# Experts on the tokens that chose them, instead of every expert on every token

## The chip, the cores and the metric

The kernel runs on one core of a Trainium2 chip. The metric is device time in microseconds (us). The kernel before takes 2458.44 us, the median of two timed runs (2458.17 and 2458.72). TensorE is called PE here, VectorE DVE, ScalarE ACT, GpSimd POOL and the queue of SyncE SP, as the profile calls them.

## The reference

Two parts are computed in fp32. A gated linear attention (4 batches, 8 heads, 768 tokens, head size 48) gives 3072 rows of 384 numbers. Then a router picks two of 8 experts for each row, and the row's result is the sum of the two experts' outputs, weighted by a softmax over the two.

```python
f = 1.0 / (1.0 + np.exp(-f_logit))
for t in range(S):
    state = f[:, :, t, :, None] * state + np.einsum('bhd,bhe->bhde', k[:, :, t], v[:, :, t])
    y[:, :, t] = np.einsum('bhd,bhde->bhe', q[:, :, t], state)
...
noisy_logits = x @ w_gate + np.log1p(np.exp(x @ w_noise)) * noise
top2 = np.argpartition(-noisy_logits, 2, axis=1)[:, :2]
...
for e in range(E):
    for k in range(2):
        mask = top2[:, k] == e
        h = np.maximum(x[mask] @ w1[e], 0.0)
        out[mask] += top2_w[mask, k, None] * (h @ w2[e])
```

An expert's w1 is 384 x 1024 and its w2 1024 x 384, 3.15 MB for both in fp32 (2 x 384 x 1024 x 4 bytes).

## The kernel before, in words

**Attention (`chunk`).** A chunk is 128 tokens of one batch for all heads. There are 6 chunks in time, each for 4 batches; two batches run by turns (a "pair"), so chunk c is two pairs. In a pair PE transposes f, q and k (L133), computes the diagonal scores (L156), then seven levels of scores (`sc`, L172). Between levels DVE merges scores (L178) and multiplies q (L182), and POOL multiplies k (`kQ`, L184) and builds the products of forget gates (`T`, L186). A level's scores wait for the level before on DVE and POOL. After the levels come the outputs y (L193, and from chunk 1 on L197 with the state), a transpose of k (L207) and the state's update (L214).

**Pack and route.** After a chunk, `pack` moves its y to a full 128-row layout xT by 10 DMAs on SP (L232), and `route` computes the logits (`lg`, L244), the two largest, and a gate for every expert that is zero beside the two (L249 to L272).

**Experts (`expert`).** Every expert runs on all six blocks of 512 tokens. A block is 24 matmuls `hp` of 128 x 512 columns (L295), each followed by a ReLU on ACT for eight of them (L297), and 32 matmuls `yp` of 384 columns (L303), which DVE weighs with the gate and adds to an accumulator in SBUF (L309). Every fp32 matmul is two records in the trace, each with its own weight load; a transpose is one. Weights come in four loads of 768 KB for each expert, issued on POOL (L279, L284). Expert 0 on block c runs between the levels of chunk c + 1, by turns; the other experts come after all chunks, in order.

**What sets the order.** A tile scheduler lists each engine's instructions, and every engine takes its list strictly in that order. An instruction that waits holds back what stands behind it on its engine. Buffers come from pools with a fixed count, and PSUM has four single banks (`ps1`) and two double ones (`ps2`).

## Time and profile before

| | us |
|---|---|
| median of the two timed runs | 2458.44 (2458.17 to 2458.72) |
| span of the profiled execution, first to last instruction | 2455.0 |
| PE busy in the span | 2401.2 (98%) |
| weight loads on PE (beside the matmuls) | 1351.6 (55%) |
| DVE busy | 406.7 (17%) |
| ACT busy | 342.7 (14%) |
| POOL busy | 223.7 (9%) |

The page gives no time of the profiled execution but its span, which is 3.4 us under the median of the timed runs. The span's engines are busy at once, so the shares do not add up to 100%. Busy PE means that records of matmuls cover the time, at either clock; how fast PE runs is read from the granted clock (PEclk, 1.00 is 2.4 GHz and 0.50 is 1.2 GHz).

### The profile page before, as it was taken

Reading aid. Unit: us, or ns where it says so; the run is one execution under the profiler, and the core shown is the slowest. Engines: PE = TensorE matmul, PEld = TensorE weight load, DVE = VectorE, ACT = ScalarE, POOL = GpSimd, SP = SyncE. Lnnn points to the kernel's source line nnn. Section 1 sums busy time; section 2 is a strip of 40 time slices with the busy share of each in tenths; the row PEclk is TensorE's granted clock in tenths of the full one; section 3 lists DMA queues with packets and bytes.
Section 4 is the critical chain, followed back from the end, with each engine's and each line's share of the span. In section 5 each row is a group of like instructions: output and inputs, shape, how many; then the busy total and the mean of one; then the engine's idle time right before and its main releaser. Section 6 shows DMA issues by size and latency. Waiting matters only on the chain.

```text
span 2455.0 us, 23370 instructions
## 1 busy us (share of the span) xinstructions
PE 2401.2 (98%) x9984; PEld 1351.6 (55%) x9984; DVE 406.7 (17%) x777; ACT 342.7 (14%) x572; POOL 223.7 (9%) x397
## 2 busy tenths in 40 slices
...
GB/s 137 66 27 40 27 40 27 40 27 33 11 55 1 0 0 52 0 0 1 52 0 1 0 52 0 1 0 52 1 0 0 52 0 0 0 26 13 26 13 26
DMA packets 113255, 55.11 MB, mean 22 GB/s; under 512 B 101792, under 2 KB 104960, under 8 KB 113152
## 3 DMA queue, kind: packets, MB, share of 16 engines
...
## 4 chain that ended last, share of the span: by engine, by line
PE 95%; POOL 2%; ACT 1%; DVE 1%; issue 1%; DMA 0%; SPq 0%; ACTq 0%; DVEq 0%; POOLq 0%
PE hp L295 41%; PE yp L303 41%; PE sc L172 6%; PE y L193 2%; PE y L197 2%; PE diag L156 1%; PE lg L244 1%; PE ds L214 1%; PE fp L133 1%; PE kp L207 1%; POOL mf L94 0%; POOL mf L92 0%; PE qp L133 0%; PE kp L133 0%; DVE qP L182 0%
## 5 line engine op out<-in xcount | busy, mean ns | idle before, releaser
L295 PE MATMUL hp<-xT,w 128*128 128x512 f32 x2304 | 1016.0, 598 | 0.0
L303 PE MATMUL yp<-w,h 128*128 128x384 f32 x3072 | 1004.3, 487 | 0.0
L303 PEld LDWEIGHTS yp<-w,h 128*128 128x128 f32 x3072 | 581.6, 190 | 412.0 <-issue 21.5
L295 PEld LDWEIGHTS hp<-xT,w 128*128 128x128 f32 x2304 | 436.7, 191 | 525.6 <-issue 511.5
L297 ACT ACTIVATE h<-hp 128x512 f32<-128x512 f32 x384 | 229.3, 597 | 1672.6 <-PE hp L295 1672.6
L309 DVE SCALAR_TENSOR_TENSOR acc<-yp,gate,acc 128x384 f32<-128x384 f32 x168 | 103.8, 618 | 1628.3 <-PE yp L303 1628.3
L172 PEld LDWEIGHTS sc<-qP,kQ 48*128 48x128 f32 (+1 forms) x2688 | 185.1, 220 | 60.1 <-issue 34.3
L172 PE MATMUL sc<-qP,kQ 48*128 48x64 f32 (+1 forms) x2688 | 197.0, 309 | 19.2 <-POOL kQ L184 12.9
L178 DVE COPY_PREDICATED A<-masks,sc 128x512 f32<-128x512 uint8 x144 | 130.0, 903 | 94.3 <-PE sc L172 80.7
L279 POOL DMA_DIRECT2D w<-in_moe_w_dram x16 | 12.2, 765 | 1383.2 <-PE hp L295 1383.2
L184 POOL TENSOR_TENSOR kQ<-kQ,T 128x256 f32<-128x256 f32 x140 | 95.2, 681 | 199.3 <-PE sc L172 198.7
L182 DVE TENSOR_TENSOR qP<-qP,T 128x256 f32<-128x256 f32 x144 | 71.5, 496 | 18.0 <-PE sc L172 17.6
L193 PE MATMUL y<-A,v 128*48 128x128 f32 x384 | 50.5, 369 | 0.0
L180 ACT COPY A<-sc 64x512 f32<-64x512 f32 x24 | 13.4, 579 | 230.6 <-DVE qP L182 225.6
L197 PE MATMUL y<-qP,st 48*48 48x128 f32 x320 | 43.5, 360 | 0.0
L156 PE MATMUL diag<-qT,kQ 48*128 48x128 f32 x384 | 33.0, 306 | 9.3 <-ACT kQ L144 9.3
L186 POOL TENSOR_TENSOR T<-T 128x128 f32<-128x128 f32 (+4 forms) x140 | 36.6, 262 | 10.0
L156 PEld LDWEIGHTS diag<-qT,kQ 48*128 48x128 f32 x384 | 26.8, 201 | 16.0 <-ACT kQ L144 15.4
L193 PEld LDWEIGHTS y<-A,v 128*48 128x48 f32 x384 | 22.4, 154 | 23.7 <-issue 22.7
L158 DVE TENSOR_TENSOR A<-diag,ident 128x1024 f32<-128x1024 f32 x24 | 29.3, 1221 | 18.0 <-PE diag L156 18.0
L200 DVE COPY yT<-y 48x512 f32<-48x512 f32 x24 | 16.7, 695 | 89.2 <-ACT yT L200 89.2
L186 POOL TENSOR_TENSOR T<-f 128x256 f32<-128x256 f32 x24 | 14.7, 614 | 174.8 <-ACT f L137 174.7
...
## 6 DMA issues: line engine op xcount, KB each, us to landing
w<-in_moe_w_dram POOLq DMA_DIRECT2D x32, 768.0 KB, 4.9
...
xT<-yT SPq DMA_DIRECT2D x36, 96.0 KB, 2.4
...
```

What stands on the lines that cost most here:

```text
L156: nc.tensor.matmul(sc[:, par, cols(hp)], lhsT=kQ[rows(par), cols(hp)], rhs=qT[rows(par), cols(hp)], start=True, stop=True)
L172: nc.tensor.matmul(sc[0:nj, par, hp * HC:(hp + 1) * HC].rearrange("j (a m) -> j a m", m=m), lhsT=kQ[rows(par), hp * C:hp * C + nj], rhs=qv ...
L178: nc.vector.copy_predicated(Av, masks[:, l].rearrange("j (r x m) -> j r x m", r=2, m=m), scv)
L182: nc.vector.tensor_tensor(qv, qv, Tv[:, :, 0:1].broadcast_to((128, x, m)), ALU.mult)
L184: nc.gpsimd.tensor_tensor(kv, kv, Tv[:, :, 1:2].broadcast_to((128, x, m)), ALU.mult)
L186: nc.gpsimd.tensor_tensor(Tn, Tv[:, :, 0], Tv[:, :, 1], ALU.mult)
L193: nc.tensor.matmul(y[rows(par), par, cols(hp)], lhsT=vt[:, 2 * hp + par, :], rhs=A[:, par, cols(hp)], start=True, stop=(c == 0))
L197: nc.tensor.matmul(y[rows(par), par, cols(hp)], lhsT=state[b][rows(par), hp, :], rhs=qP[rows(par), cols(hp)], start=False, stop=True)
L295: nc.tensor.matmul(hp, lhsT=w[:, i, o:o + 128], rhs=xT[c][:, i, :], start=(i == 0), stop=(i == KO - 1))
L297: nc.scalar.activation(hs, hp, AF.Relu)
L303: nc.tensor.matmul(yp[:, 0:DM], lhsT=h[fo][:, b * C:(b + 1) * C], rhs=w2[fo // HALF][:, fo % HALF, :], start=(fo == 0), stop=(fo == FO - 1))
L309: nc.vector.scalar_tensor_tensor(a, in0=yp[:, 0:DM], scalar=g, in1=a, op0=ALU.mult, op1=ALU.add)
```

## The change

The experts no longer run on all tokens. Each expert has a list in DRAM of the tokens that chose it, and work is done in blocks of 128 list slots: 55 blocks, (2 x 3072 - 8) // 128 + 8, enough for any choice of the router.

- At the start 24 DMAs on POOL write zeros to the output, and one DMA on SP fills the lists with empty slots.
- `route` also transposes the chunk's rows back to token rows and stores them in DRAM (`x_rows`). It counts, by two matmuls (`rk`), at which slot of its expert's list each token comes, and writes eight times 128 list entries by indirect DMAs on POOL (`lists`). An entry is: token, token again if an earlier expert has written its output row (else an address out of range), weight, token.
- `plan`, once after all chunks, computes for each of the 55 blocks the expert, the list row and whether weights must be loaded (`steer`).
- Per block SP reads three numbers of `steer` into registers, loads the block's 128 entries (`slots`), and loads w1 and w2 under a condition into one of three buffers in turn; after a change of expert all three are loaded anew, so 24 of the 55 pairs of loads are made if every expert has three blocks or more. POOL gathers 128 rows of x (`xg`), PE turns them (`xgp`), computes 24 matmuls of 128 columns (`hp`) and 8 of 384 (`yp`). POOL gathers what the output rows held (`had`), DVE adds, and POOL scatters the rows to the output (`ys`). A gather of `had` waits until the scatter of the block before has landed.

```diff
-    HALF = FO // 2
+    NB = (2 * N - E) // 128 + E
+    NR = 3
+    FAR = 1 << 20
     assert (H * D, H * DP, 1 << NL, B * S) == (DM, 512, C, N) and TB == 512
...
-    wts = ctx.enter_context(tc.tile_pool(name="wts", bufs=3))
-    hid = ctx.enter_context(tc.tile_pool(name="hid", bufs=10))
+    ffn = ctx.enter_context(tc.tile_pool(name="ffn", bufs=3))
...
-    iota = const.tile([128, E], F32, tag="iota", name="iota")
-    nc.gpsimd.iota(iota, pattern=[[1, E]], base=0, channel_multiplier=0, allow_small_or_imprecise_dtypes=True)
+    iota = counting("iota", [[1, E]])
+    list_of = counting("list_of", [[N, E]])
+    token = counting("token", [[C, NCH], [S, B]], by_partition=1)
+    start_of = counting("start_of", [[128, N // 128]])
+    block = counting("block", [[1, NB]])
+    ones = const.tile([128, 128], F32, tag="ones", name="ones")
+    nc.gpsimd.memset(ones, 1.0)
+    earlier = const.tile([128, 128], F32, tag="earlier", name="earlier")
+    nc.gpsimd.affine_select(out=earlier, in_=ones, compare_op=ALU.is_ge, fill=0.0, base=-1,
+                            pattern=[[1, 128]], channel_multiplier=-1)
+    LR = E * N + 128
+    x_rows = tc.dram_tile([N, DM], F32, name="x_rows")
+    lists = tc.dram_tile([LR, 4], U32, name="lists")
+    empty = const.tile([128, LR // 128, 4], U32, tag="empty", name="empty")
+    for i, val in enumerate((0, FAR, 0, FAR)):
+        nc.vector.memset(empty[:, :, i], val)
+    nc.sync.dma_start(out=lists.rearrange("(p r) w -> p r w", p=128), in_=empty)
...
-    xT = [const.tile([128, KO, TB], F32, tag=f"xT{c}", name=f"xT{c}") for c in range(NCH)]
-    acc = [const.tile([128, B, DM], F32, tag=f"acc{c}", name=f"acc{c}") for c in range(NCH)]
-    gate = [const.tile([128, B, E], F32, tag=f"gate{c}", name=f"gate{c}") for c in range(NCH)]
+    xT = [None] * NCH
+    before = const.tile([128, NCH * B + 1, E], F32, tag="before", name="before")
+    nc.vector.memset(before[:, 0, :], 0.0)
...
     def route(c):
+        for b in range(B):
+            xp = one_bank(f"xp_{c}_{b}")
+            for i in range(KO):
+                nc.tensor.transpose(xp[:, i * 128:(i + 1) * 128], xT[c][:, i, b * C:(b + 1) * C], ident)
+            xs = t([DM], "xs")
+            nc.scalar.copy(xs, xp[:, 0:DM])
+            nc.sync.dma_start(out=x_rows[b * S + c * C:b * S + (c + 1) * C, :], in_=xs)
         lg = one_bank(f"lg_{c}")[:, 0:B * 2 * E].rearrange("t (b e) -> t b e", b=B)
...
-        hot = [t([B, E], "hot0"), t([B, E], "hot1")]
+        hot = [t([B, E], f"hot{r}") for r in range(2)]
         for r in range(2):
             nc.vector.tensor_tensor(hot[r], iota.unsqueeze(1).broadcast_to((128, B, E)),
                                     fx[:, :, r:r + 1].broadcast_to((128, B, E)), ALU.is_equal)
-            nc.vector.tensor_tensor(hot[r], hot[r], ex[:, :, r:r + 1].broadcast_to((128, B, E)), ALU.mult)
-        nc.vector.tensor_tensor(gate[c], hot[0], hot[1], ALU.add)
-    # ---- one expert on one block of tokens ----
-    def load_expert(e):
-        w1, w2 = [], []
-        for s in range(2):
-            w = wts.tile([128, KO, HALF * 128], F32, tag="w1", name=f"w1_{e}_{s}")
-            nc.gpsimd.dma_start(out=w, in_=moe_w1[e, :, s * HALF * 128:(s + 1) * HALF * 128].rearrange(
-                "(k p) f -> p k f", p=128))
...
-        return w1, w2
-    def expert(e, c, w1, w2):
-        h = []
+        both = t([B, E], "both")
+        nc.vector.tensor_tensor(both, hot[0], hot[1], ALU.add)
+        for b in range(B):
+            n = c * B + b
+            nc.vector.tensor_tensor(before[:, n + 1, :], before[:, n, :], both[:, b, :], ALU.add)
+        rk = one_bank(f"rk_{c}")[:, 0:B * E].rearrange("t (b e) -> t b e", b=B)
+        nc.tensor.matmul(rk, lhsT=earlier, rhs=both, start=True, stop=False)
+        nc.tensor.matmul(rk, lhsT=ones, rhs=before[:, c * B:(c + 1) * B, :], start=False, stop=True)
+        at = t([B, E], "at")
+        nc.vector.tensor_tensor(at, rk, list_of.unsqueeze(1).broadcast_to((128, B, E)), ALU.add)
+        late = t([B, 2], "late")
+        nc.vector.tensor_tensor(late[:, :, 0:1], fx[:, :, 0:1], fx[:, :, 1:2], ALU.is_gt)
+        nc.vector.tensor_tensor(late[:, :, 1:2], fx[:, :, 1:2], fx[:, :, 0:1], ALU.is_gt)
+        entry = t([B, 2, 4], "entry", U32)
+        tok = token[:, c, :].unsqueeze(2).broadcast_to((128, B, 2))
...
+        nc.vector.tensor_scalar(entry[:, :, :, 1], prev, float(FAR), None, ALU.add)
+        nc.vector.tensor_copy(entry[:, :, :, 0], tok)
...
+        nc.vector.tensor_copy(entry[:, :, :, 2].bitcast(F32), ex)
+        slot, sloti = t([2, B], "slot"), t([2, B], "sloti", U32)
+        for r in range(2):
+            nc.vector.tensor_tensor(hot[r], hot[r], at, ALU.mult)
+            nc.vector.tensor_reduce(slot[:, r, :], hot[r], axis=AX.X, op=ALU.add)
+        nc.vector.tensor_copy(sloti, slot)
+        for b in range(B):
+            for r in range(2):
+                put = nc.gpsimd.indirect_dma_start(
+                    out=lists, out_offset=bass.IndirectOffsetOnAxis(ap=sloti[:, r, b:b + 1], axis=0),
+                    in_=entry[:, b, r, :], in_offset=None)
+                tc.declare_no_dep(put.ins, group="lists", reason="slots differ")
+                tc.add_to_no_dep_group("lists", put.ins)
+    def plan():
+        def t(shape, tag, dtype=F32):
+            return rt.tile([128] + shape, dtype, tag=tag, name=tag, bufs=1)
+        total = one_bank("total")[:, 0:E]
+        nc.tensor.matmul(total, lhsT=ones, rhs=before[:, NCH * B, :], start=True, stop=True)
+        full = t([E, N // 128], "full")
+        nc.vector.tensor_tensor(full, total.unsqueeze(2).broadcast_to((128, E, N // 128)),
+                                start_of.unsqueeze(1).broadcast_to((128, E, N // 128)), ALU.is_gt)
+        nblk, upto = t([E], "nblk"), t([E], "upto")
+        nc.vector.tensor_reduce(nblk, full, axis=AX.X, op=ALU.add)
...
+        past = t([NB, E], "past")
...
+        ex, off = t([NB], "bex"), t([NB], "off")
+        nc.vector.tensor_reduce(ex, past, axis=AX.X, op=ALU.add)
...
+        row = t([NB], "row")
+        nc.vector.scalar_tensor_tensor(row, in0=ex, scalar=float(N), in1=off, op0=ALU.mult, op1=ALU.add)
...
+        steer = t([NB, 4], "steer", I32)
...
+        new = t([NB], "new")
+        nc.vector.memset(new[:, 0:NR], 1.0)
+        nc.vector.tensor_tensor(new[:, NR:], ex[:, NR:], ex[:, 0:NB - NR], ALU.not_equal)
+        nc.vector.tensor_copy(steer[:, :, 2], new)
+        nc.vector.tensor_copy(steer[:, :, 3], new)
+        return steer
+    w1 = [const.tile([128, KO, FF], F32, tag=f"w1_{i}", name=f"w1_{i}") for i in range(NR)]
+    w2 = [const.tile([128, FO, DM], F32, tag=f"w2_{i}", name=f"w2_{i}") for i in range(NR)]
+    def fetch(t, steer):
+        slots = ffn.tile([128, 4], U32, tag="slots", name=f"slots{t}", bufs=6)
+        e, row, new = (nc.values_load(steer[0:1, t, i:i + 1], engines=[mybir.EngineType.SP], min_val=0, max_val=hi,
...
+                       for i, hi in ((0, E - 1), (1, E * N), (2, 1)))
+        nc.sync.dma_start(out=slots, in_=lists[bass.ds(row, 128), :])
+        xg = ffn.tile([128, DM], F32, tag="xg", name=f"xg{t}", bufs=4)
+        nc.gpsimd.indirect_dma_start(out=xg, out_offset=None, in_=x_rows,
+                                     in_offset=bass.IndirectOffsetOnAxis(ap=slots[:, 0:1], axis=0))
+        return slots, xg, e, new
+    def weights(t, e, new):
+        i = t % NR
+        nc.sync.dma_start(out=w1[i], in_=moe_w1[bass.ds(e, 1)].rearrange("o (k p) f -> p (o k) f", p=128), cond=new)
+        nc.sync.dma_start(out=w2[i], in_=moe_w2[bass.ds(e, 1)].rearrange("o (f p) d -> p (o f) d", p=128), cond=new)
+    def turned(t, xg):
+        xp = one_bank(f"xgp{t}")
+        for i in range(KO):
+            nc.tensor.transpose(xp[:, i * 128:(i + 1) * 128], xg[:, i * 128:(i + 1) * 128], ident)
+        xt = ffn.tile([128, KO, 128], F32, tag="xt", name=f"xt{t}")
+        nc.vector.tensor_copy(xt, xp[:, 0:DM].rearrange("d (k t) -> d k t", k=KO))
+        return xt
+    def hidden(t, xt):
+        hp = two_banks(f"hp{t}").rearrange("f a (o t) -> f a o t", t=128)
+        hs = ffn.tile([128, FO, 128], F32, tag="hs", name=f"hs{t}")
         for fo in range(FO):
-            hp = one_bank(f"hp_{e}_{c}_{fo}")
-            w, o = w1[fo // HALF], (fo % HALF) * 128
             for i in range(KO):
-                nc.tensor.matmul(hp, lhsT=w[:, i, o:o + 128], rhs=xT[c][:, i, :], start=(i == 0), stop=(i == KO - 1))
-            hs = hid.tile([128, TB], F32, tag="h", name=f"h_{e}_{c}_{fo}")
-            nc.scalar.activation(hs, hp, AF.Relu)
-            h.append(hs)
-            yield
-        for b in range(B):
-            yp = one_bank(f"yp_{e}_{c}_{b}")
-            for fo in range(FO):
-                nc.tensor.matmul(yp[:, 0:DM], lhsT=h[fo][:, b * C:(b + 1) * C], rhs=w2[fo // HALF][:, fo % HALF, :],
-                                 start=(fo == 0), stop=(fo == FO - 1))
-            a, g = acc[c][:, b, :], gate[c][:, b, e:e + 1]
...
-                nc.vector.scalar_tensor_tensor(a, in0=yp[:, 0:DM], scalar=g, in1=a, op0=ALU.mult, op1=ALU.add)
...
-            yield
+                nc.tensor.matmul(hp[:, fo // 4, fo % 4, :], lhsT=w1[t % NR][:, i, fo * 128:(fo + 1) * 128],
+                                 rhs=xt[:, i, :], start=(i == 0), stop=(i == KO - 1))
+            if fo % 4 == 3:
+                nc.scalar.activation(hs[:, fo - 3:fo + 1, :], hp[:, fo // 4], AF.Relu)
+        return hs
+    def result(t, hs, slots):
+        had = ffn.tile([128, DM], F32, tag="had", name=f"had{t}")
+        nc.gpsimd.memset(had, 0.0)
+        nc.gpsimd.indirect_dma_start(out=had, out_offset=None, in_=out,
+                                     in_offset=bass.IndirectOffsetOnAxis(ap=slots[:, 1:2], axis=0),
+                                     bounds_check=N - 1, oob_is_err=False)
+        yp = one_bank(f"yp{t}")
+        for fo in range(FO):
+            nc.tensor.matmul(yp[:, 0:DM], lhsT=hs[:, fo, :], rhs=w2[t % NR][:, fo, :],
+                             start=(fo == 0), stop=(fo == FO - 1))
+        ys = ffn.tile([128, DM], F32, tag="ys", name=f"ys{t}")
+        nc.vector.scalar_tensor_tensor(ys, in0=yp[:, 0:DM], scalar=slots[:, 2:3].bitcast(F32), in1=had,
+                                       op0=ALU.mult, op1=ALU.add)
+        nc.gpsimd.indirect_dma_start(out=out, out_offset=bass.IndirectOffsetOnAxis(ap=slots[:, 3:4], axis=0),
+                                     in_=ys, in_offset=None, bounds_check=N - 1, oob_is_err=False)
...
+    zero = const.tile([128, DM], F32, tag="zero", name="zero")
+    nc.vector.memset(zero, 0.0)
+    for i in range(0, N, 128):
+        nc.gpsimd.dma_start(out=out[i:i + 128, :], in_=zero)
     load_router()
     for c in range(NCH):
         yT[c] = wk.tile([128, HP, B, C], F32, tag="yT", name=f"yT{c}", bufs=1)
-        by_turns(chunks(c, range(0, B, 2)), chunks(c, range(1, B, 2)), expert(0, c - 1, *w) if c else ())
-        if c == 0:
-            w = load_expert(0)
+        by_turns(chunks(c, range(0, B, 2)), chunks(c, range(1, B, 2)))
+        xT[c] = wk.tile([128, KO, TB], F32, tag="xT", name=f"xT{c}")
         pack(c)
         route(c)
-    for e in range(E):
-        if e:
-            w = load_expert(e)
-        for c in range(NCH) if e else (NCH - 1,):
-            by_turns(expert(e, c, *w))
+    steer = plan()
+    AHEAD = 3
+    got = {}
+    def begin(t):
+        got[t] = fetch(t, steer)
+        weights(t, *got[t][2:])
+    for t in range(AHEAD):
+        begin(t)
+    xt = {0: turned(0, got[0][1])}
+    for t in range(NB):
+        hs = hidden(t, xt.pop(t))
+        if t + AHEAD < NB:
+            got[t + AHEAD] = fetch(t + AHEAD, steer)
+        if t + 1 < NB:
+            xt[t + 1] = turned(t + 1, got[t + 1][1])
+        result(t, hs, got[t][0])
+        if t + AHEAD < NB:
+            weights(t + AHEAD, *got[t + AHEAD][2:])
```

Three places show how the instructions stand. The first is PE between the last update of the state in chunk 0 and the first levels of chunk 1, before (`lg` is the logits, `fp`, `qp` and `kp` the transposes of chunk 1):

```order
L214 MATMUL ds_3_815<-v_3_536,kn_3_813 64x48 x8
L244 MATMUL lg_844<-w_rt,xT_137 128x16
L133 MATMUL fp_0_899<-ident,f_85 128x128 x4
L133 MATMUL qp_0_906<-ident,q_88 128x128 x4
L133 MATMUL kp_0_915<-ident,k_91 128x128 x4
L133 MATMUL fp_1_938<-ident,f_86 128x128 x4
L156 MATMUL diag_0_922<-qT_0_905,kQ_0_914 128x128 x5
L244 MATMUL lg_844<-w_rt,xT_137 128x16
L156 MATMUL diag_0_922<-qT_0_905,kQ_0_914 128x128 x3
```

And now:

```order
L277 MATMUL xp_2_886<-ident,xT_861 128x128
L277 MATMUL xp_3_893<-ident,xT_861 128x128
L285 MATMUL lg_900<-w_rt,xT_861 128x16 x12
L320 MATMUL rk_951<-both_945,earlier 128x32
L166 MATMUL fp_0_989<-ident,f_82 128x128 x3
L321 MATMUL rk_951<-before,ones 128x32
L166 MATMUL fp_0_989<-ident,f_82 128x128
L166 MATMUL qp_0_996<-ident,q_85 128x128 x4
L166 MATMUL kp_0_1005<-ident,k_88 128x128 x4
```

Before, the logits were slipped in between the transposes of the next chunk; now the three transposes for each batch, all logits and the count `rk`, which needs the whole of the router's chain on ACT and DVE, stand ahead of the first transpose of chunk 1.

The second is POOL after the last k product of chunk 0, before:

```order
L184 TENSOR_TENSOR kQ_2_497<-kQ_2_497,T_0_2_724 128x4x64
L184 TENSOR_TENSOR kQ_3_554<-kQ_3_554,T_0_3_738 128x4x64
L186 TENSOR_TENSOR T_1_0_989<-f_0_898 128x256
L186 TENSOR_TENSOR T_1_0_1023<-T_1_0_989 128x128
L186 TENSOR_TENSOR T_1_0_1057<-T_1_0_1023 128x64
L186 TENSOR_TENSOR T_1_0_1091<-T_1_0_1057 128x32
```

And now:

```order
L217 TENSOR_TENSOR kQ_2_532<-kQ_2_532,T_0_2_759 128x4x64
L217 TENSOR_TENSOR kQ_3_589<-kQ_3_589,T_0_3_773 128x4x64
L343 DMA lists<-entry_959,sloti_968 24704x4 x8
L219 TENSOR_TENSOR T_1_0_1073<-f_0_988 128x256
L219 TENSOR_TENSOR T_1_1_1087<-f_1_1027 128x256
L219 TENSOR_TENSOR T_1_0_1101<-T_1_0_1073 128x128
```

The eight indirect DMAs of chunk 0's list entries (`x8`) now stand ahead of everything that POOL does for chunk 1.

The third is POOL in the middle of the 55 blocks, now (there is nothing of this kind before; `slots_6131` is the list entries of one block, `slots_6199` those of the next):

```order
L426 DMA had_6354<-out_dram,slots_6131 128x384
L395 DMA xg_6278<-x_rows,slots_6267 128x384
L436 DMA out_dram<-ys_6368,slots_6131 3072x384
L425 MEMSET had_6558 128x384
L426 DMA had_6422<-out_dram,slots_6199 128x384
L395 DMA xg_6346<-x_rows,slots_6335 128x384
L436 DMA out_dram<-ys_6436,slots_6199 3072x384
L425 MEMSET had_6626 128x384
```

For each block POOL has a gather of old output rows, the gather of x for the block two further on, the scatter, and a memset, in this order.

## Rows read from the trace of the kernel before

**Rows 1.** Engine busy time by stretch: us, busy PE PEld DVE ACT POOL, PEclk, DMA, GB/s.

```profile
0.00:58.60 58.60, 38.34 (x312) 34.01 (x312) 26.08 (x40) 6.56 (x10) 51.84 (x71) 1.00 0.82 144
58.60:94.70 36.10, 33.48 (x354) 31.29 (x352) 20.82 (x34) 6.52 (x12) 14.26 (x28) 0.67 0.28 45
94.70:671.30 576.60, 550.47 (x4482) 367.35 (x4480) 250.42 (x506) 119.75 (x199) 137.87 (x272) 0.88 0.19 32
671.30:2455.00 1783.70, 1778.90 (x4840) 918.91 (x4840) 109.34 (x198) 209.85 (x351) 19.69 (x26) 1.00 0.04 15
```

**Rows 2.** Chain that ended last: start us, us, what; an expert block after chunks.

```profile
698.54 20.64 PE yp L303 x64
719.18 20.60 PE hp L295 x48
```

**Rows 3.** Costliest groups, shapes apart (busy us, mean ns | idle before).

```profile
L295 PE MATMUL hp<-xT,w 128*128 128x512 f32 x2304 | 1016.0, 598 | 0.0
L303 PE MATMUL yp<-w,h 128*128 128x384 f32 x3072 | 1004.3, 487 | 0.0
...
L309 DVE SCALAR_TENSOR_TENSOR acc<-yp,gate,acc 128x384 f32<-128x384 f32 x168 | 103.8, 618 | 1628.3 <-PE yp L303 1628.3
...
L197 PE MATMUL y<-qP,st 48*48 48x128 f32 x320 | 43.5, 360 | 0.0
```

**Rows 4.** Timeline of TensorE, full-row transposes in chunk 4: start us, us, what.

```profile
505.12 0.60 PE L133 MATMUL qp<-ident,q 128*128 128x128 f32 x4
505.56 0.60 PE L133 MATMUL kp<-ident,k 128*128 128x128 f32 x4
```

**Rows 5.** Timeline of TensorE, the first pair of chunk 0.

```profile
31.38 3.83 PE L172 MATMUL sc<-qP,kQ 48*128 48x64 f32 x32 [11.13 <-POOL kQ L184]
...
55.04 3.65 PE L193 MATMUL y<-A,v 128*48 128x128 f32 x32
```

**Rows 6.** Timeline of TensorE, second pair of chunk 0.

```profile
69.96 20.51 PE L172 MATMUL sc<-qP,kQ 48*128 48x64 f32 x192 [0.49 <-DVE A L158]
...
91.68 3.10 PE L193 MATMUL y<-A,v 128*48 128x128 f32 x32
```

**Rows 7.** Timeline of all engines, from chunk 5's last y to its gates.

```profile
667.57 0.67 PE L197 MATMUL y<-qP,st 48*48 48x128 f32 x4
...
668.89 6.31 SPq L232 DMA_DIRECT2D xT<-yT  x10
...
678.98 2.30 PE L244 MATMUL lg<-w_rt,xT 128*128 128x16 f32 x20
...
688.34 0.19 DVE L272 TENSOR_TENSOR gate<-hot,hot 128x32 f32<-128x32 f32 x1
```

**Rows 8.** Groups of POOL, shapes apart.

```profile
L279 POOL DMA_DIRECT2D w<-in_moe_w_dram x16 | 12.2, 765 | 1383.2 <-PE hp L295 1383.2
...
L92 POOL TENSOR_SCALAR_AFFINE_SELECT mf<-mf 128x512 f32<-128x512 f32 x6 | 10.8, 1796 | 0.0
L94 POOL TENSOR_SCALAR_AFFINE_SELECT mf<-mf 128x512 f32<-128x512 f32 x6 | 10.7, 1790 | 0.0
...
L353 POOL MEMSET const-float32-0.0<- 128x1 f32 x1 | 0.1, 100 | 0.3 <-issue 0.3
```

**Rows 9.** Timeline of POOL: the dearest instruction of the run.

```profile
6.78 4.08 POOL L94 TENSOR_SCALAR_AFFINE_SELECT mf<-mf 128x512 f32<-128x512 f32 x1
```

**Rows 10.** Timeline of POOL, a tree of forget products in chunk 1.

```profile
100.51 0.61 POOL L186 TENSOR_TENSOR T<-f 128x256 f32<-128x256 f32 x1 [7.77 <-ACT f L137]
...
101.20 1.95 POOL L186 TENSOR_TENSOR T<-T 128x128 f32<-128x128 f32 x6
```

**Rows 11.** Page, part 6: DMA issues, KB each, us to landing.

```profile
w<-in_moe_w_dram POOLq DMA_DIRECT2D x32, 768.0 KB, 4.9
...
xT<-yT SPq DMA_DIRECT2D x36, 96.0 KB, 2.4
```

**Rows 12.** Half a microsecond inside a weight load; last column GB/s.

```profile
723.00:723.50 0.50, 0.50 (x3) 0.26 (x2) 0.00 (x0) 0.00 (x0) 0.00 (x0) 1.00 1.06 433
```

More of the change, by code (lines that the diff above doesn't have):

```diff
@@ L11 @@
 U32 = mybir.dt.uint32
+I32 = mybir.dt.int32
 AF = mybir.ActivationFunctionType
+AX = mybir.AxisListType
 ALU = mybir.AluOpType
@@ L96, with counting @@
         nc.gpsimd.tensor_copy(masks[:, l], mf)
-    iota = const.tile([128, E], F32, tag="iota", name="iota")
-    nc.gpsimd.iota(iota, pattern=[[1, E]], base=0, channel_multiplier=0, allow_small_or_imprecise_dtypes=True)
+    def counting(name, pattern, base=0, by_partition=0):
+        t = const.tile([128] + [n for _, n in pattern], F32, tag=name, name=name)
+        nc.gpsimd.iota(t, pattern=pattern, base=base, channel_multiplier=by_partition,
+                       allow_small_or_imprecise_dtypes=True)
+        return t
+    iota = counting("iota", [[1, E]])
[15 more added lines that the diff above has]
+    nc.sync.dma_start(out=lists.rearrange("(p r) w -> p r w", p=128), in_=empty)
     w_rt = const.tile([128, KO, 2 * E], F32, tag="w_rt", name="w_rt")
@@ new lines, in route @@
+        at = t([B, E], "at")
[5 more added lines that the diff above has]
+        tok = token[:, c, :].unsqueeze(2).broadcast_to((128, B, 2))
+        prev = t([B, 2], "prev")
+        nc.vector.tensor_scalar(prev, tok, -float(FAR), None, ALU.add)
@@ new lines, in route @@
+        nc.vector.tensor_tensor(prev, prev, late, ALU.mult)
+        nc.vector.tensor_scalar(entry[:, :, :, 1], prev, float(FAR), None, ALU.add)
+        nc.vector.tensor_copy(entry[:, :, :, 0], tok)
+        nc.vector.tensor_copy(entry[:, :, :, 3], tok)
+        nc.vector.tensor_copy(entry[:, :, :, 2].bitcast(F32), ex)
[3 more added lines that the diff above has]
+            nc.vector.tensor_reduce(slot[:, r, :], hot[r], axis=AX.X, op=ALU.add)
@@ new lines, in route @@
+        nc.vector.tensor_copy(sloti, slot)
[16 more added lines that the diff above has]
+        nc.vector.tensor_reduce(nblk, full, axis=AX.X, op=ALU.add)
+        nc.vector.tensor_tensor_scan(upto, data0=ones[:, 0:E], data1=nblk, initial=0.0, op0=ALU.mult, op1=ALU.add)
+        past = t([NB, E], "past")
+        nc.vector.tensor_tensor(past, block.unsqueeze(2).broadcast_to((128, NB, E)),
+                                upto.unsqueeze(1).broadcast_to((128, NB, E)), ALU.is_ge)
+        ex, off = t([NB], "bex"), t([NB], "off")
+        nc.vector.tensor_reduce(ex, past, axis=AX.X, op=ALU.add)
+        nc.vector.tensor_tensor(past, past, nblk.unsqueeze(1).broadcast_to((128, NB, E)), ALU.mult)
+        nc.vector.tensor_reduce(off, past, axis=AX.X, op=ALU.add)
+        nc.vector.tensor_tensor(off, block, off, ALU.subtract)
+        nc.vector.tensor_scalar(off, off, 128.0, None, ALU.mult)
+        row = t([NB], "row")
+        nc.vector.scalar_tensor_tensor(row, in0=ex, scalar=float(N), in1=off, op0=ALU.mult, op1=ALU.add)
+        steer = t([NB, 4], "steer", I32)
+        nc.vector.tensor_scalar(steer[:, :, 1], row, float(E * N), None, ALU.min)
+        nc.vector.tensor_scalar(ex, ex, float(E - 1), None, ALU.min)
+        nc.vector.tensor_copy(steer[:, :, 0], ex)
+        new = t([NB], "new")
[4 more added lines that the diff above has]
+        return steer
```

12 lines of the change are left out of this document (1 added, 11 removed).

## The prediction

> **What bounds the kernel now.** I read the windows by stage first [rows 1]: in the last 1,783.70 us PE is busy 1,778.90 at a granted clock of 1.00, while DMA is at 0.04. That stretch is nothing but expert blocks: 43 of them, which the chain [rows 2] shows as 20.60 us of `hp` and 20.64 us of `yp` in turn, with no wait. The groups [rows 3] say the same over the run: the two expert lines hold 2,020 us, and DVE's add idles behind PE. The stretch before it (94.7 to 671.3) has PE busy 550.47 of 576.60 us, but at clock 0.88: five chunks of recurrence, mixed with the first five expert blocks, which fill PE where levels wait. The timelines [rows 5, 6] give a pair of blocks alone: 36.10 us [rows 1].
>
> The profiled span is 2,455.0 us; the median of the runs is 3.4 above it, so I add 3 to a sum on the span.
>
> **The experts, per block.** One block had 512 tokens; now it has 128 slots. An `hp` record was 20.60/48 = 0.429 us for 512 columns, so 0.107 for 128; the nearest row of 128 columns with a weight load for each record is the transposes [rows 4], 0.44 us for 4. I take 0.109: 48 x 0.109 = 5.23 us. `yp` keeps its 384 columns: 16 records of 20.64/64 = 0.3225 make 5.16. Three transposes at 0.11 add 0.33. **PE: 10.7 us a block, 55 blocks 589 us**, against 48 x 41.24 = 1,980 before: two choices of eight experts are a quarter of the work, and the rest is partly filled blocks.
>
> What must hide behind 10.7 us:
> - *Weights.* 24 pairs of loads of 3.15 MB (four of the 768 KB transfers [rows 11]) at the 433 GB/s of [rows 12] take 7.3 us each; a block's time suffices down to 291 GB/s. They are issued three blocks ahead at best, as soon as `yp` frees the buffer. If cover fails here, PE waits for the load: I add 1 us (0 to 2) to each of the 24. `slots` stands behind them on SP's queue, but is also fetched three blocks ahead. If the condition should not skip anything, 55 loads take 400 us of DMA in 589 us, and still hide.
> - *SP's reads of three numbers into registers* have no row; bounded by 0 below and by the three blocks, 32 us, above, I take 0.
> - *The chain through the output.* On POOL a block issues `had`'s gather, the gather of `xg`, the scatter of `ys`, and `had` may go only when the scatter before has landed. Call p POOL's time for one indirect DMA and L the time from its end to landing: one round is 2p + 2L + DVE's 0.62 + about 0.3 of hand-overs. No row has p. Below is the plain issue, 0.77 us [rows 8]; above is POOL's dearest instruction, 4.08 [rows 9]. An indirect DMA is an issue that also reads 128 addresses, so I take it nearer the first row, at twice that: p = 1.5. L: a 786 KB load lands 4.9 us after its issue began [rows 11]; less the issue (0.77) and 786 KB at 433 GB/s (1.8) 2.3 remain, and 197 KB add 0.45: 2.8. The round is then 9.5 us, hidden by 10.7; it decides from p = 2.1.
> - The eviction of the second half of `hp` has eight `yp` records, 2.6 us, ahead of its use.
>
> **The start.** On POOL all mask work, `iota`s, the 24 zero stores and six loads now stand ahead of the first `kQ`. The two mask groups take 21.5 us [rows 8], 30 issues at 0.765 take 23, the memsets, casts and counters about 8 (an estimate): level 1 begins near 55 instead of 31.4 [rows 5]. Six levels at the second pair's pace, 20.5, its `y` 3.1 [rows 6] and hand-overs end the first pair at 81 instead of 58.7; the second, 36.1 later: **117**.
>
> **The chunks.** Expert 0 leaves their gaps. Ten groups of four of line 197 take 4.35 us [rows 3] per pair: 36.1 + 4.4 = 40.5, two pairs 81 per chunk.
>
> **The route.** It moves into the way. `rk` on PE stands ahead of the next chunk's first transposes and waits for the whole gate chain; on POOL eight list scatters stand ahead of the next chunk's trees and `kQ`, and wait for slot numbers. From chunk 5 [rows 7]: last `y` ends 668.24, the ten pack DMAs are issued by 675.20, `lg` ends 681.28, gates 688.53: 20.3 us. Counting, `rk` and two `xs` copies add about 3 (some twelve operations like the 0.19 us one of [rows 7], and hand-overs): slots at +23.3. Then 8p = 12, two trees 2 x 2.56 [rows 10], `kQ` 0.8: level 1 at +41.2. Between the first pair's `y` (58.69) and the next level 1 (69.96) lay 11.3 [rows 5, 6]. So each chunk but the last loses 41.2 - 11.3 = **30 us**, five times. The stores of `x_rows` ride SP's queue ahead of loads needed a pair later, 36 us; were that cover gone, four issues like those of `xT` [rows 7], 0.63 each, would cost 2.5 a chunk.
>
> **Sum.** Last `y` at 117 + 5 x (81 + 30) = 672. Slots +23.3, eight scatters +12, landing +2.5; `plan`'s twenty small DVE operations hide behind the scatters: 710. `slots` 2.4 [rows 11], a gather 4.3, turning 1: 718; the first weights, issued as `steer` is ready, end near 722; the first block, at a cold clock, takes 5 more: 727. 55 blocks: 1,316. Loads +24, last add, scatter and landing +5, and +3: **1,348 us**. Of the gain, about 1,390 comes from the experts; 280 goes back, half of it in the route.
>
> **Rivals.**
>
> *A. The chain through the output sets the pace* (p above 2.1, or longer landing while weights move). For it: everything in the loop is latency, and PE's 10.7 is just above it. Against: nothing but the bound. At p = 3 the round is 12.5 us: 55 x 1.8 = 99 more, and 60 in 40 list scatters: 1,507. At 4.08 it is 14.7: 220 + 103 more, 1,671.
>
> *B. Weight loads show.* With 128 columns a record lasts no longer than its weight load may. If the load runs alone, 48 x 0.107 = 5.1 us more a block: 283, total 1,631. Each of the transposes' records speaks against it: each of those records loads 128 rows anew, in 0.11 us together [rows 4]. The Trainium skill, page "TensorE: Matmul & The Clock Gate", section on packing small matmuls, says that a weight load overlaps matmuls in flight only when its row group differs; all of these use all rows, so by that rule it would be this case, 1,631; the trace speaks against it, and it has only a small chance.
>
> *C. The blocks run at 1.2 GHz.* Where PE waited on levels the clock was 0.67 and 0.88 [rows 1]; in pure expert work it was 1.00. If waits in each block (weights, gathers) keep it at the lower level, a block takes 21.4: 1,348 + 589 = 1,937. But waits of a tenth are what I forecast, not of a third.
>
> *D. Slower than before: POOL writes the addresses of an indirect DMA one by one.* Then p is 128 times the time for one. The shortest POOL instruction takes 0.10 us [rows 8]: p = 12.8. Once p exceeds L, POOL's three indirect DMAs and one landing make the round, 3p + L + 0.9, and 40 list scatters stand on the path: the total is about 870 + 209p, here 3,545. It crosses 2,455 at p = 7.6, or 59 ns for an address, and is clearly slower from 7.8. The rows neither show nor exclude it; no POOL instruction but those with 512 columns lasts above 2 us. The Trainium skill, page "GPSIMD Engine Reference", section on performance pitfalls for Q7 kernels, says that many small read commands, such as one for each gather index, cost some 102 cycles each without overlap; estimated at 1.2 GHz that gives 10.9 us, total 3,150. No run so far shows it.
>
> **How the numbers follow.** PE-paced blocks 0.55, at 1,348; A 0.25; B 0.04; C 0.05; D 0.06; 0.05 for something unlisted, mostly shorter. The first case's own range is 1,250 (p = 0.77 saves 29, loads cost nothing 24, a route shorter by 8 us 40) to 1,440 (p = 2.1 costs 24, loads 24, route and start 45). The range takes in A to its end and B: 1,240 to 1,680; C and D lie outside, as does what is unlisted. Two per cent either way, 49 us, is about what the measurement cannot tell from no change; only a p between about 7.4 and 7.8 lands there: 0.01. Slower is D, 0.06; faster the rest, 0.93.
>
> **What would show it.** In the profile after: PE's `hp` of a block near 5.2 us and `yp` near 5.2, and block starts 10.7 apart; the mean of POOL's indirect DMAs, which is p (1.5 here; above 2.1 A, above 7.6 D); PE's idle time ahead of `xgp`, `hp` and `yp`, and who ends it: SP's queue for weights, POOL's for gathers; DVE's add waiting for `had` and not for `yp` would mean A. `hp` near 10 at clock 1.00 is B; all at half speed with a clock of 0.5 to 0.67 is C. In the chunks, 41 us from the last `y` of one to level 1 of the next with the releaser on POOL; level 1 of the first at 55. It would be wrong above all if an indirect DMA has a price outside 0.77 to 4.08, or lands much later than a plain one.

## The result, and the profile after

The changed kernel takes 1,419.0 us (1,414.2 to 1,423.9), 0.577 of the time before, with an interval of 0.573 to 0.582. The forecast was 1,348, in a range of 1,240 to 1,680; the main case's own range was 1,250 to 1,440. The profiled execution took 1,423.9. One execution in e3 (2,618 us, the traced one) and one in e14 (1,331.7 us) were slow and are left out of the times below.

By stage (columns as in [rows 1]): one chunk, the gap between recurrence and blocks, and all blocks.

```profile
112.00:230.00 118.00, 93.65 (x810) 76.63 (x807) 48.55 (x114) 21.01 (x36) 35.75 (x64) 0.57 0.22 42
...
692.00:738.00 46.00, 10.82 (x48) 9.01 (x46) 9.36 (x56) 6.88 (x12) 9.91 (x10) 0.50 0.25 80
738.00:1415.00 677.00, 625.64 (x3685) 494.11 (x3685) 64.05 (x109) 65.67 (x110) 185.51 (x214) 0.98 0.44 146
```

PE is busy for 92% of the blocks' time at nearly full clock (0.98, where [rows 1] has 1.00), but the clock in the chunks fell from 0.88 to 0.57. From the last `y` of chunk 0 to the last `y` of chunk 5, five chunks with expert 0 in their gaps took 573.5 us (94.78 to 668.24); without it, and with the route in the way, they take 583.1 (109.64 to 692.70).

The groups (columns as in [rows 3]):

```profile
L417 PE MATMUL hp<-xt,w 128*128 128x128 f32 x2640 | 327.5, 282 | 23.9 <-ACT hs L420 23.3 <-DVE xt L409 0.7
...
L431 PE MATMUL yp<-w,hs 128*128 128x384 f32 x880 | 294.6, 488 | 0.0
...
L426 POOL DMA_INDIRECT had<-out_dram,slots x55 | 57.0, 1036 | 174.6 <-issue 138.3 <-DMA out_dram<-ys,slots 35.6 <-POOL had L425 0.7
L436 POOL DMA_INDIRECT out_dram<-ys,slots x55 | 55.6, 1011 | 295.8 <-DVE ys L434 295.4 <-issue 0.3
...
L343 POOL DMA_INDIRECT lists<-entry,sloti x48 | 46.9, 977 | 208.6 <-DVE sloti L340 195.8 <-issue 12.8
...
L407 PE MATMUL xgp<-ident,xg 128*128 128x128 f32 x165 | 29.7, 291 | 49.5 <-DMA xg<-x_rows,slots 49.5
```

An indirect DMA of 128 addresses holds POOL for 1.0 us. PE waits in two places: 48 times for ACT in the middle of `hp`, and 12 times for a gather of `xg` (the first of these, 22.7 us, ahead of the first block). The timeline of PE shows the wait for ACT in an undisturbed block (compare [rows 2]):

```profile
784.54 2.84 PE L417 MATMUL hp<-xt,w 128*128 128x128 f32 x24
788.12 2.94 PE L417 MATMUL hp<-xt,w 128*128 128x128 f32 x24 [0.75 <-ACT hs L420]
790.91 0.49 PE L407 MATMUL xgp<-ident,xg 128*128 128x128 f32 x3
791.23 5.33 PE L431 MATMUL yp<-w,hs 128*128 128x384 f32 x16
796.40 2.84 PE L417 MATMUL hp<-xt,w 128*128 128x128 f32 x24
```

This block takes 11.86 us (784.54 to 796.40). From the tenth block on the three transposes `xgp` stand in that wait and no longer behind `hp`, and blocks start 11.53 us apart. Over 54 starts (738.64 to 1,394.55) 11.53 makes 622.6 of 655.9 us; the other 33.3 come in the first blocks and where an expert changes. POOL and PE at such a place:

```profile
957.40 1.01 POOL L436 DMA_INDIRECT out_dram<-ys,slots  x1 [5.81 <-DVE ys L434]
...
966.70 1.04 POOL L426 DMA_INDIRECT had<-out_dram,slots  x1 [7.86 <-issue]
968.04 0.97 POOL L395 DMA_INDIRECT xg<-x_rows,slots  x1 [0.31 <-PE yp L431]
...
974.61 0.90 PE L407 MATMUL xgp<-ident,xg 128*128 128x128 f32 x3 [3.94 <-DMA xg<-x_rows,slots]
975.31 4.01 PE L417 MATMUL hp<-xt,w 128*128 128x128 f32 x24
```

`had`'s gather starts 9.3 us after the scatter before it. The row names no releaser (`issue`); by the program it waits for that scatter to land, and scatters land between 2.2 and 8.2 us after their issue began, 2.6 in the median. `xg`, of which PE has need first, stands behind `had`. The wait costs PE more than its 3.94 us: the 24 records after it take 4.01 us instead of 2.84. Between two chunks the timeline of PE answers to [rows 7]:

```profile
237.47 2.75 PE L285 MATMUL lg<-w_rt,xT 128*128 128x16 f32 x12
...
249.22 0.61 PE L320 MATMUL rk<-both,earlier 128*128 128x32 f32 x2 [6.46 <-DVE late L326]
...
257.77 1.01 PE L205 MATMUL sc<-qP,kQ 48*128 48x64 f32 x16
268.08 20.70 PE L205 MATMUL sc<-qP,kQ 48*128 48x64 f32 x192 [9.30 <-DVE A L191]
```

`rk` waits for the gates. Then POOL issues eight list scatters, 1.27 us apart, and only after them the trees; DVE's state update waits for these, and the product `A`, for which PE's next level waits, stands behind that. POOL and DVE there:

```profile
252.06 1.01 POOL L343 DMA_INDIRECT lists<-entry,sloti  x1 [33.15 <-DVE sloti L340]
...
261.00 0.97 POOL L343 DMA_INDIRECT lists<-entry,sloti  x1 [0.30 <-issue]
261.99 1.19 POOL L219 TENSOR_TENSOR T<-f 128x256 f32<-128x256 f32 x2
...
265.63 1.27 DVE L254 TENSOR_TENSOR st<-st,T 128x192 f32<-128x192 f32 x2 [8.79 <-POOL T L219]
266.82 1.21 DVE L191 TENSOR_TENSOR A<-diag,ident 128x1024 f32<-128x1024 f32 x1
```

### The profile page after: what moved, and what is told of

The parts are those of the page before. It is cut to its first block, busy times and chain, and to the rows that moved or that the text cites. A ratio compares the mean times of both kernels' runs of the same rounds, so it can differ in the third digit from the quotient of the medians.

```text
span 1422.2 us, 21155 instructions
## 1 busy us (share of the span) xinstructions
PE 1178.9 (83%) x8391; PEld 953.1 (67%) x8391; DVE 357.8 (25%) x814; ACT 189.6 (13%) x322; POOL 448.1 (32%) x663
## 5 line engine op out<-in xcount | busy, mean ns | idle before, releaser
L417 PEld LDWEIGHTS hp<-xt,w 128*128 128x128 f32 x2640 | 317.6, 197 | 49.9 <-ACT hs L420 34.5
L417 PE MATMUL hp<-xt,w 128*128 128x128 f32 x2640 | 327.5, 282 | 23.9 <-ACT hs L420 23.3
L205 PE MATMUL sc<-qP,kQ 48*128 48x64 f32 (+1 forms) x2688 | 274.0, 392 | 82.4 <-DVE A L191 43.3
L205 PEld LDWEIGHTS sc<-qP,kQ 48*128 48x128 f32 (+1 forms) x2688 | 263.2, 301 | 93.0 <-DVE A L191 44.7
L431 PE MATMUL yp<-w,hs 128*128 128x384 f32 x880 | 294.6, 488 | 0.0
L431 PEld LDWEIGHTS yp<-w,hs 128*128 128x128 f32 x880 | 163.7, 191 | 102.9 <-issue 1.7
L420 ACT ACTIVATE hs<-hp 128x512 f32<-128x512 f32 x110 | 65.7, 597 | 631.3 <-PE hp L417 623.7
L436 POOL DMA_INDIRECT out_dram<-ys,slots x55 | 55.6, 1011 | 295.8 <-DVE ys L434 295.4
L426 POOL DMA_INDIRECT had<-out_dram,slots x55 | 57.0, 1036 | 174.6 <-issue 138.3
L407 PE MATMUL xgp<-ident,xg 128*128 128x128 f32 x165 | 29.7, 291 | 49.5 <-DMA xg<-x_rows,slots 49.5
L215 DVE TENSOR_TENSOR qP<-qP,T 128x256 f32<-128x256 f32 x144 | 62.2, 432 | 11.3 <-PE sc L205 10.4
L395 POOL DMA_INDIRECT xg<-x_rows,slots x55 | 53.4, 971 | 30.7 <-issue 19.4
```

The costliest lines, as they stand in the source:

```text
L205: nc.tensor.matmul(sc[0:nj, par, hp * HC:(hp + 1) * HC].rearrange("j (a m) -> j a m", m=m), lhsT=kQ[rows(par), hp * C:hp * C + nj], rhs=qv ...
L215: nc.vector.tensor_tensor(qv, qv, Tv[:, :, 0:1].broadcast_to((128, x, m)), ALU.mult)
L395: nc.gpsimd.indirect_dma_start(out=xg, out_offset=None, in_=x_rows, in_offset=bass.IndirectOffsetOnAxis(ap=slots[:, 0:1], axis=0))
L417: nc.tensor.matmul(hp[:, fo // 4, fo % 4, :], lhsT=w1[t % NR][:, i, fo * 128:(fo + 1) * 128], rhs=xt[:, i, :], start=(i == 0), stop=(i == ...
L420: nc.scalar.activation(hs[:, fo - 3:fo + 1, :], hp[:, fo // 4], AF.Relu)
L426: nc.gpsimd.indirect_dma_start(out=had, out_offset=None, in_=out, in_offset=bass.IndirectOffsetOnAxis(ap=slots[:, 1:2], axis=0), bounds_ch ...
```

## The experiments

Each result is the median in us, its ratio to the kernel before, and the interval of that ratio. The changed kernel timed again is the base of all that follows: **1,419.8**, 0.578 (0.576 to 0.579).

> The changed kernel itself, timed in more rounds as the base for the others. Both theories: the same as before, 1,414 to 1,424 us, ratio 0.577; block starts 11.53 us apart where no expert changes.

**e1: `hp` in two tiles.**

```diff
-        hp = two_banks(f"hp{t}").rearrange("f a (o t) -> f a o t", t=128)
+        hp = [two_banks(f"hp{t}_{a}")[:, 0].rearrange("f (o t) -> f o t", t=128) for a in range(2)]
...
```

> The two halves of hp lie in two PSUM tiles instead of one. In the profile after, the second half starts 0.69 to 0.75 us after the first ends, released by ACT. Theory: that wait is for the ReLU's read of the first half, because both halves are one tile; it goes, block starts come 10.78 apart instead of 11.53, and 55 x 0.75 = 41 us go: 1,378. Rival 1 (the chain through the output sets the pace of 11.53): PE waits elsewhere instead, block starts stay at 11.5, time stays at 1,419. Rival 2 (the wait is something else that ACT does): nothing changes either, and the gap stays in the middle of hp.

Measured **1,551.2**, 0.631 (0.630 to 0.632): slower than the base, which neither the theory nor a rival had forecast. The timeline of PE:

```profile
1007.96 5.52 PE L417 MATMUL hp<-xt,w 128*128 128x128 f32 x48
...
1034.03 0.90 PE L407 MATMUL xgp<-ident,xg 128*128 128x128 f32 x3 [6.91 <-DMA xg<-x_rows,slots]
1034.73 7.12 PE L431 MATMUL yp<-w,hs 128*128 128x384 f32 x16
```

The gap in `hp` is gone, as the theory said. But the edit also changed the planned order on POOL: the gather of `xg` for block t+1 now stood beside `had` of block t, where it had been t+2. PE waited for 54 gathers, 174 us in all, against 49.5 in the base. Its own work slowed as well: behind a long wait 16 records of `yp` take 7.12 us instead of 5.33, and over all blocks the granted clock is 0.92 with PE busy for 651 us, against 0.99 and 601 in e11. The run doesn't tell the split from the new order; e11 does.

**e2: weights loaded three times only.** In the comparison that makes `new`, the operand `ex[:, 0:NB - NR]` became `ex[:, NR:]`. The kernel leaves out the later experts' weights.

> The condition is never true after the first three blocks: 3 pairs of weight loads instead of 24 (the experts after the first compute with the first three buffers' weights). Theory (the 33 us by which 54 block starts exceed 54 x 11.53 are late landings while 3.15 MB loads move): all blocks 11.53 apart, 1,420 - 30 = 1,390. Rival (the late gathers come from the queue on POOL or the slots DMA behind the weights in SP's program, moving or not): the irregular blocks stay, 1,410 to 1,420.

Measured **1,394.4**, 0.567 (0.566 to 0.568). The waits of PE for `xg` (total us, times, longest; 49.5, 12, 22.7 in the kernel after):

```profile
PE xgp L407 <- DMA xg<-x_rows,slots: 27.2, 2, 22.6
```

Starts are 11.5 apart from the tenth block on, and the 54 starts exceed 54 x 11.53 by 4.7 us instead of 33.3. So the late gathers come from the loads.

**e3: gathers one block further ahead.**

```diff
-        if t + AHEAD < NB:
-            got[t + AHEAD] = fetch(t + AHEAD, steer)
+        if t + MORE < NB:
+            got[t + MORE] = fetch(t + MORE, steer)
...
```

`MORE` is 5; the weights keep `AHEAD`, which is 3.

> slots and xg are fetched five blocks ahead in the program instead of three (nine and six buffers; hs has two instead of three); on POOL the gather of xg then stands three blocks ahead of its use instead of two, still behind had. The weight loads stay. Theory (PE waits only because xg's gather is queued behind had's, which waits for the scatter's landing that a weight load stretches from 2.4 to 8 us; one block more of lead covers that): the waits for xg of 27 us go, 1,393. Rival (the chain scatter, had, add, scatter itself is too long in those blocks): waits move to yp's PSUM or the add, 1,415 to 1,420.

Measured **1,387.9**, 0.564 (0.563 to 0.565), with all loads in place: the theory's time. No timeline shows where its waits went; e11 has the same lead.

**e5: no gather of `had`** (`had` stays zero).

> The gather of had is left out (tokens keep only the contribution of their later expert), so no step of a block waits for a scatter to land and xg stands on POOL with no wait ahead of it but the scatter's for the add. Theory (PE sets the pace, the chain through the output only delays xg in weight blocks): steady blocks stay at 11.53, the 27 us of waits for xg go: 1,393. Rival (the chain through the output sets the pace of all blocks): block starts fall to 10.8 or less in steady blocks, 1,350.

Measured **1,398.7**, 0.570 (0.569 to 0.571), and starts are still 11.5 apart. The waits of PE for `xg`:

```profile
PE xgp L407 <- DMA xg<-x_rows,slots: 29.0, 7, 22.5
```

So the chain through the output doesn't set the pace of the steady blocks; it delays `xg` where weights move.

**e11: e1 and e3 together.**

> hp in two PSUM tiles as in e1, and slots and xg five blocks ahead as in e3, so that xg stands three blocks ahead on POOL, where e1 had left it one block ahead. Theory (e1 lost because its gathers were issued one block ahead of use instead of two; the gap in hp is a separate 0.75 us): starts 10.78 apart, 1,420 - 41 - 25 = 1,354. Rival (without the gap PE is faster than the chain through the output, which takes over, as in e1): 1,400 to 1,550.

Measured **1,351.7**, 0.549 (0.548 to 0.550). The timeline of PE has no gap:

```profile
1007.72 0.49 PE L410 MATMUL xgp<-ident,xg 128*128 128x128 f32 x3
1008.05 5.52 PE L420 MATMUL hp<-xt,w 128*128 128x128 f32 x48
1013.41 5.33 PE L434 MATMUL yp<-w,hs 128*128 128x384 f32 x16
1018.57 0.49 PE L410 MATMUL xgp<-ident,xg 128*128 128x128 f32 x3
```

Starts are 10.85 apart. Against e3 the split is worth 36 us, so e1 lost by its gathers and not by the split.

**e6: zero stores on SP** (`nc.sync` for `nc.gpsimd` at line 454).

> The 24 zero stores of the output go out on SP's queue instead of POOL's. In the profile after, POOL issues them for 13.4 us ahead of the first kQ and level 1 starts at 48.5. Theory (POOL's order is what the start waits for): level 1 at about 35, and 13 us less: 1,406. Rival (the start is bound by the loads that the stores collide with): the stores now stand ahead of the loads of v and of the second block on SP's queue, level 1 stays at 45 to 50 or later, no gain, up to 10 us loss.

Measured **1,405.9**, 0.572 (0.571 to 0.573), the theory's sum. Its place was half right. Level 1, in the base and here:

```profile
48.49 3.68 PE L205 MATMUL sc<-qP,kQ 48*128 48x64 f32 x32 [27.39 <-POOL kQ L217]
...
42.06 18.20 PE L205 MATMUL sc<-qP,kQ 48*128 48x64 f32 x166 [8.62 <-POOL kQ L217]
```

Level 1 starts at 42.1 and not at 35. POOL is busy up to there: in the new order both trees of `T` and three memsets of `had`, 6 us, stand ahead of the first `kQ`, where the base had them behind it and PE waited at level 2 instead (2.58 us). The last `y` of chunk 0 ends 9.1 us earlier (100.5, 109.6 in the base). The other 5 us were not traced to a place, and four runs of the base differ by 7.5, so the close agreement of the sum is in part luck.

**e7: the route in two pieces** (`route(c - 1)` after the first pair of chunk c, a new `enlist(c - 1)` from `rk` on after the second).

> The route of a chunk is done in two pieces, out of the way of the recurrence: gates after the next chunk's first pair, rk and the list scatters after its second pair. Theory (the chunks of 117 us are two pairs of 45.7 and a stall of 26, since rk on PE and the list scatters on POOL stand ahead of the next chunk's work and wait for the gate chain): chunk pace about 95, five times 22 us less: 1,310; the transposes and lg stay on PE, 8 us, so not all of 26 goes. Rival (POOL and DVE are needed by the levels anyway, the eight scatters of 1.27 us stop kQ and the gates stop the level's selects): half of it comes back as longer pairs, 1,360 to 1,419.

Measured **1,397.5**, 0.569 (0.568 to 0.570), the rival's time. Chunks take 116 (117.6 in the base); from pair to pair it is 56 to 61 us, where the base had 45.7 and 72 by turns. POOL in the second gap:

```profile
223.48 0.61 POOL L219 TENSOR_TENSOR T<-f 128x256 f32<-128x256 f32 x1 [16.94 <-ACT f L170]
224.31 1.09 POOL L346 DMA_INDIRECT lists<-entry,sloti  x1 [0.21 <-issue]
...
233.36 0.97 POOL L346 DMA_INDIRECT lists<-entry,sloti  x1 [0.30 <-issue]
234.35 0.62 POOL L219 TENSOR_TENSOR T<-f 128x256 f32<-128x256 f32 x1
```

All eight scatters stand between the first steps of the two trees. PE's wait ahead of `rk` went, but the issue time stayed in the path.

**e10: the route spread over the levels** (`route` and `enlist` become streams beside the two of `by_turns`, a piece a turn; each scatter is held behind the level's `kQ`).

> The route of a chunk is spread over the levels of the next: transposes, logits and gates one piece for each level of the first pair, slot numbers and one list scatter behind each level's kQ in the second pair. In the chunks of the split route (e7) the pace was 116 us, 57 to 58 a pair: ACT's copies and gates stood between the pairs, and ten us of scatters ahead of the trees. Theory (those engines have free time inside the levels, ACT almost all of it, POOL 1.1 us a level): pairs of 45.7 plus the 8 us of PE work and little else, a chunk 100 to 104, five times 14 less: 1,350. Rival (the levels have no room either: DVE is busy 70% of them and a scatter of 1.27 us is longer than POOL's gap of 1.07): 110 to 116 a chunk, 1,385 to 1,415.

Measured **1,344.5**, 0.547 (0.546 to 0.549), the theory. `rk` follows `rk` 103 us apart, without a wait but in the last chunk. POOL:

```profile
182.79 0.84 POOL L218 TENSOR_TENSOR kQ<-kQ,f 128x256 f32<-128x256 f32 x1 [1.19 <-PE sc L206]
183.80 1.09 POOL L358 DMA_INDIRECT lists<-entry,sloti  x1 [0.16 <-issue]
184.92 0.74 POOL L218 TENSOR_TENSOR kQ<-kQ,T 128x256 f32<-128x256 f32 x1
```

**e9: filler in the chunks.**

```diff
+    def filler(c):
+        for i in range(24):
+            fp = one_bank(f"fill{c}_{i}")
+            for j in range(2):
+                nc.tensor.matmul(fp, lhsT=ident, rhs=fill, start=(j == 0), stop=(j == 1))
+            yield
...
```

`filler(c)` is a third stream beside the two of `by_turns`; `hs` has two buffers instead of three.

> 48 matmuls of 512 columns that nobody reads are added to each of the six chunks, two at each level and twelve where PE waits for the packed rows: 96 records, 41.2 us a chunk at 0.429 us each, as much PE work as expert 0 had there before the change. Theory (the chunks did not get shorter when expert 0 left them, 115 us each with it, 117 without, since the levels then run at clock 0.50): with filler the clock in the chunks rises to 0.8 or more, the levels' own records fall from 0.108 us towards 0.06, and the chunks stay within 110 to 125 us; total 1,400 to 1,470. Rival (PE time adds up): 41 us more a chunk, 1,420 + 247 = 1,667.

Measured **1,457.5**, 0.593 (0.592 to 0.594): 247 us more PE work cost 38. A window of one chunk, and one level with its filler:

```profile
230.00:350.00 120.00, 102.29 (x869) 64.90 (x868) 46.85 (x110) 20.54 (x36) 34.63 (x62) 0.91 0.22 41
...
290.51 2.02 PE L205 MATMUL sc<-qP,kQ 48*128 48x64 f32 x32
292.46 1.98 PE L458 MATMUL fill<-fill,ident 128*128 128x512 f32 x4
```

The 32 records of a level take 2.0 us and not 3.45 (20.67/6), and a pair's `y` 5.7 and not 9.6. A chunk of 117.6 us grows by 7.5 to 125.1. Little of the filler lies in time when PE was idle anyway: PE idles 24.4 of 118 us without it and 17.7 of 120 with it. The rest is paid by the clock.

**e13: e11, e6 and e10 in one.**

> e11, e6 and e10 in one kernel: hp in two tiles, gathers five blocks ahead in the program, zero stores on SP, the route spread over the levels. If the terms are separate they add: 1,420 - 68 - 14 - 70 = 1,268, and with the rival of e10 1,300 to 1,335. If they cover each other, no better than e11, 1,352.

Measured **1,262.8**, 0.514 (0.513 to 0.514): the terms add, 68 + 14 + 75 = 157 us. It is the fastest of the kernels here, 11% below the changed one.

**e14: e13 with less filler** (one matmul a turn, 18 a chunk).

> The kernel with everything (e13, 1,263 us, 103 us a chunk) and one unread matmul of 512 columns for each turn of the recurrence, 18 a chunk, 15.5 us of PE work at the higher clock (ys has two buffers instead of three). Theory (the levels are bound by PE records of 0.108 us at clock 0.50, which fall to 0.062 under filler as in e9, and 0.86 us of filler a turn costs less than the 1.4 us that 32 records then save): a turn of the two blocks falls from 3.44 to about 2.9 us, y and the transposes go with the clock: 8 to 15 us a chunk, 1,180 to 1,215. Rival (so little filler does not raise the clock): 15.5 to 31 us a chunk more, 1,350 to 1,450. Between (clock raised, but DVE's 2.7 us a turn and the route's pieces take over): 1,240 to 1,270.

Measured **1,315.5**, 0.534 (0.533 to 0.535): 53 slower than e13 and outside all three ranges. The clock, 0.57 in these stretches of e13, rises in some of them only:

```profile
200.00:300.00 100.00, 97.38 (x666) 66.20 (x664) 37.41 (x93) 15.86 (x27) 27.25 (x45) 0.59 0.16 33
300.00:400.00 100.00, 92.01 (x834) 62.81 (x832) 49.13 (x114) 20.56 (x35) 36.16 (x64) 0.80 0.28 49
```

Two stretches of PE's timeline, at the higher level and at the lower:

```profile
324.56 2.03 PE L206 MATMUL sc<-qP,kQ 48*128 48x64 f32 x32
326.52 1.12 PE L476 MATMUL fill<-fill,ident 128*128 128x512 f32 x2
...
382.11 3.68 PE L206 MATMUL sc<-qP,kQ 48*128 48x64 f32 x32
385.72 2.07 PE L476 MATMUL fill<-fill,ident 128*128 128x512 f32 x2
```

At the lower level a filler matmul costs 2.0 us a level and gives nothing back. What decides between the two is not shown.

## Why the prediction held, and which terms were off

The sum against the profiled execution:

| part | forecast | measured |
|---|---|---|
| to the last `y` of chunk 0 | 117 | 110 |
| five chunks | 555 | 583 |
| to the first `xgp` | 45 | 46 |
| 55 blocks | 623 | 676 |
| end | 8 | 9 |
| sum | 1,348 | 1,424 |

The forecast's first `xgp` starts at 710 + 2.4 + 4.3 = 717; its blocks hold all from there to the last 8 us.

The prediction held: the 55 blocks, paced by PE, brought the gain, and the main case's range was wide enough for two terms that came out larger. The room in that range was meant for p, the loads, the route and the start, and most of the excess came from elsewhere.

- **Blocks (+53).** PE sets the pace, and its own work is near the forecast's 10.7 (10.85 in e11, 8 us in all). The step that failed is "the eviction of the second half has eight `yp` records ahead of its use": it names only that eviction. The second half's matmuls also wait until ACT has read the first half, because both lie in one tile; that was put at nothing. e11 against e3 shows it: 0.68 a block, some 37 us.
- **Loads.** 24 us were added for PE waiting for weights. PE never waited for them; instead the loads delay a scatter's landing, this `had`, and this `xg` (e2, e3, e5). Some 29 of the 33 us go when the loads go (e2). That is rival A, but only in blocks around the loads. Elsewhere its round is short: scatter and gather land 2.6 and 3.0 us after their issue began, p is 1.0 of that and not 1.5, and with 0.9 for the add 6.5 us are used of 11.5.
- **Chunks (+28).** From the last `y` of a chunk to level 1 of the next the forecast was 41.2 us, and 40.6 were measured (227.52 to 268.08). That agreement is in part luck: slots came at 24.5 and not 23.3, the scatters took 9.9 and not 12, the trees 3.7 and not 5.1, and 1.4 of DVE's state update and `A` stood behind, which was not foreseen. The step that was mis-sized is the pair: 45.7, not 40.5, since `y` takes 9.6 instead of 7.45 and 14.2 instead of 11.3 pass from `y` to level 1. (So the route costs 117.6 - 2 x 45.7 = 26 and not 30.) Both had been priced from [rows 1, 3, 5, 6] with expert work or the run's start beside them. (The 4.35 us of line 197 are eight groups of four and not ten; ten pairs share the 43.5 us of [rows 3].) Without that work the clock is 0.50 in the levels and 0.64 from `y` to the next level 1:

```profile
150.00:172.00 22.00, 21.44 (x208) 20.85 (x208) 15.39 (x26) 0.58 (x1) 8.21 (x12) 0.50 0.01 2
172.00:196.00 24.00, 21.25 (x182) 14.04 (x179) 6.92 (x12) 6.24 (x11) 5.96 (x16) 0.64 0.41 67
```

- **Rival C.** I had it look for a low clock in the blocks only, and set it aside with "waits of a tenth are what I forecast, not of a third". No row has such a third: at clock 0.67 PE idled 2.6 of 36.1 us [rows 1]. The low clock was in the chunks. e9 shows its price: with as much PE work put back as expert 0 had, a chunk is only 7.5 us longer, so taking expert 0 out of the chunks could give little back.
- **Start (-7).** Level 1 began at 48.5 and not 55. The zero stores take 0.56 us each, not 0.765, which is 5 of the 6.5 us. Taking them off POOL is worth 14 us on the whole (e6).
- **B and D fell.** 48 records in 5.52 us are 0.115 each, weight load included. The rule of the Trainium skill ("TensorE: Matmul & The Clock Gate", packing small matmuls) would give twice that; the measurement decides against it for these matmuls. 128 addresses cost 1.0 us. The estimate from the Trainium skill's page "GPSIMD Engine Reference" (performance pitfalls for Q7 kernels), 10.9 us, does not apply to these DMAs.

What stays open is why a scatter lands late beside weight loads. Behind the scatter of 957.40 the DMA engines are busy for 0.93 of the time and move 301 GB/s:

```profile
957.50:966.00 8.50, 8.08 (x53) 6.52 (x52) 0.56 (x1) 1.19 (x2) 1.34 (x2) 1.00 0.93 301
```

Until 961.4 no packet of the scatter moves, while in a quiet block (issue at 934.33) its packets begin 1.2 us after the issue. So most of the delay lies ahead of its first packet. No run separates shared bandwidth from the order in the DMA queues.
